# Denominators of a sketched attention from extra sketch columns instead of extra matmuls, and no early squares on GpSimd

## The chip, the cores and the metric

The kernel runs on one core of one Trainium2 chip. The metric is device time in microseconds (us) of one launch. Runs come with a state; a run more than 1.5% above the fastest of its kernel is called slow and is left out of comparisons.

## The reference, cut to what matters

Four batches of a polynomial-sketch attention (4 heads, 1088 positions, head size 32, r = 8) feed a feed-forward layer (FFN) with a squared ReLU.

```python
def phi(x):                         # q and k: 64 features per position
    a = np.einsum('rd,bhsd->bhsr', S1, x)
    b = np.einsum('rd,bhsd->bhsr', S2, x)
    return np.einsum('bhsi,bhsj->bhsij', a, b).reshape(*x.shape[:-1], r * r)
q_p, k_p = phi(q), phi(k)
kv = np.einsum('bhsf,bhsd->bhfd', k_p, v)
z = np.sum(k_p, axis=2)
num = np.einsum('bhsf,bhfd->bhsd', q_p, kv)
den = np.einsum('bhsf,bhf->bhs', q_p, z)[..., None] + 1e-06
x = num / den                       # 4352 tokens of 128
h = np.maximum(x @ w_in, 0.0)       # 2048 wide
out = h * h @ w_out
```

The identity behind the change: the denominator is the sum over i of a_i times the sum over j of z_ij b_j. The inner sum is linear in q, so it can be had from eight more columns of the q sketch, with weights z times S2.

## The kernel before

TensorE does a pair of matmuls per FFN block and token chunk: `pg` (x times w_in, one record in the trace) and `po` (times w_out, float32, two records); at 384 tokens they take 0.17 and 0.65 us of the chain. ScalarE does the ReLU (`gt`), and ScalarE, VectorE or, early on, GpSimd the square (`g`). Meanwhile each batch's attention is prepared. A small list scheduler in the kernel (`O`) fixes the order of instructions on each engine at build time from estimated durations. The path of a batch is: `kT`, `kc`, `fs`, `kp`, `ks` (k features) - `kvp` (kv and z) - `kvt`, copies `kv`, `z` on GpSimd; and `qT`, `qc` (q sketch) - `qb`, `qa` shuffles out of PSUM - `qp` products - `nd` (numerators and denominators) - `dT`, `dn`, `rd`, `bc` - `xT`.

```python
def a_kvr(b, h):                                   # GpSimd, per head
    ...
    for c in range(4):
        nc.gpsimd.tensor_copy(_ap(st[b, "kv"], 32 * c, 32, 64 * h, ...), _ap(st["kvt"], ...))
        nc.gpsimd.tensor_copy(_ap(zs[b % 2], 32 * c, 32, 64 * h + 8 * c, ...), _ap(st["kvt"], ...))

def a_qc(b, i0, nb):                               # q sketch, 16 small matmuls
    sketch(st[b, "qc", i0], qT, 32 * i0, 8 * nb, sf[:, 64:96])   # columns 16-31 of sf's part are zero

def a_nd(b, i0, nb, nd=None, col=0):
    ...                                            # numerators: 32 matmuls, kv x qp
    for o_, m0, w in dens(m):                      # denominators: z x qp
        for e in range(E):
            for h in range(H):
                nc.tensor.matmul(nd[32 * h : 32 * h + 32, col + o_ : col + o_ + w],
                                 z[:, o : o + 32], st[b, "qp", i0, e][:, ...], ...)

def a_dn(b, i0, nb):                               # VectorE: transpose, + eps, reciprocal
    ...

# squares: the first on VectorE, then ScalarE or VectorE, and GpSimd too for u < 9
{"DVE": dve(w)} if u < ND else {"ACT": 0.095 + w / 1200, "DVE": dve(w), **PS[u < NP]}

# bulk loads of batch b (k, v, q)
s0 = tu[first_unit[b - 1, 0]] - 8.0 if b > 1 else 0.0
```

A float32 matmul is two records in these traces, so the 16 calls of `sketch` show as `qc` x32.

Of the kernel before, what the change touches and what calls it, by code (L numbers as in the profile page):

```python
# [14 lines left out]
def _ap(t: bass.AP, p0: int, np_: int, off: int, free):  # L15
    p = list(t.ap)[0]
    return bass.AP(
        t.tensor, t.offset + p0 * p[0] + off, [[p[0], np_]] + [list(d) for d in free]
    )


class _Order:
# [30 lines left out]
    def run(self, hop=0.25):  # L53
        free = {}
        todo = list(self.ops)
        for op in todo:
            for e in op["engs"]:
                free.setdefault(e, 0.0)
        t = 0.0
        while todo:  # L60
            later, done = [], []
            for e in free:
                if free[e] > t:
                    later.append(free[e])
                    continue
                best = None
                for op in todo:
                    if e not in op["engs"] or op["start"] is not None:
                        continue
                    if any(d["end"] is None for d in op["deps"]):  # L70
                        continue
                    if any(d["start"] is None or d["start"] >= t for d in op["soft"]):
                        continue
                    r = op["at"]
                    for d in op["deps"]:
                        r = max(r, d["end"] + (0.0 if d["eng"] == e else hop + op["lag"]))
                    r += op["late"].get(e, 0.0)
                    if r > t:
                        later.append(r)
                    elif best is None or op["key"] < best["key"]:  # L80
                        best = op
                if best is not None:
                    best["start"], best["eng"] = t, e
                    best["end"] = free[e] = t + best["engs"][e]
                    done.append(best)
                    later.append(free[e])
            if done:
                todo = [op for op in todo if op["start"] is None]
            t = min((x for x in later if x > t), default=t + 0.01)
            assert t < 1000.0, [op["name"] for op in todo][:20]  # L90
        for op in sorted(self.ops, key=lambda op: (op["start"], op["n"])):
            op["emit"](op["eng"])
# [3 lines left out]
def kernel(  # L96
# [19 lines left out]
    GT, G2, LA = 4, 6, 3.5  # L116
    LU = 4
    W0, W3 = 10, 3
    ND, WI, KL = 1, (2.0, 4.0), (30.0, 8.0)



# [30 lines left out]
    kT, qT = sb("kT", SP), sb("qT", SP)  # L153
    w_in32, w_o, w_in = sb("w_in32", 2048), sb("w_o", 2048), sb("w_in", 2048, F32R)
    s_nat, s_T = sb("s_nat", 32, rows=32), sb("s_T", 32, rows=32)
    zs = [sb(f"z{i}", 64 * H) for i in range(2)]


    def load_k(eng, b, c0=0, c1=S):
# [256 lines left out]

    def a_rep_z(t_, col):
        nc.vector.tensor_tensor(
            out=_ap(zs[0], 0, 128, 0, [[32, 4], [128, 2], [1, 32]]),
            in0=_ap(t_, 0, 128, col + 32, [[512, 4], [64, 2], [1, 32]]),  # L420
            in1=_ap(own_c, 0, 128, 0, [[0, 4], [0, 2], [1, 32]]),
            op=mult,
        )


    def a_kvr(b, h):
        if h == 0:
            st[b, "kv"] = bpool.tile([128, 64 * H], F32, tag="kv", name="kv")
        for c in range(4):
            nc.gpsimd.tensor_copy(  # L430
                _ap(st[b, "kv"], 32 * c, 32, 64 * h, [[32, E], [1, 32]]),
                _ap(st["kvt"], 32 * h, 32, 0, [[64, E], [1, 32]]),
            )
            nc.gpsimd.tensor_copy(  # L434
                _ap(zs[b % 2], 32 * c, 32, 64 * h + 8 * c, [[32, E], [1, 8]]),
                _ap(st["kvt"], 32 * h, 32, 32, [[64, E], [1, 8]]),
            )

    def a_qc(b, i0, nb):
        st[b, "qc", i0] = att("qc")  # L440
        sketch(st[b, "qc", i0], qT, 32 * i0, 8 * nb, sf[:, 64:96])

    def a_qs(b, i0, nb, which, x):
        m = 8 * nb
# [24 lines left out]
    def a_nd(b, i0, nb, nd=None, col=0):  # L469
        m = 8 * nb  # L470
        nd = att("nd") if nd is None else nd
        st[b, "nd", i0] = nd, col
        kv, z = st[b, "kv"], zs[b % 2]
        for e in range(E):
            qp = st[b, "qp", i0, e]
            ch = [(c, h) for c in range(4) for h in range(H)]
            for c, h in ch:
                r, o = slice(32 * c, 32 * c + 32), 64 * h + 32 * e
                nc.tensor.matmul(  # L479
                    nd[32 * h : 32 * h + 32, 512 * c + col : 512 * c + col + m],  # L480
                    kv[r, o : o + 32], qp[r, m * h : m * h + m],
                    start=(e == 0), stop=(e == 1),
                )
        for o_, m0, w in dens(m):
            for e in range(E):
                for h in range(H):
                    o = 64 * h + 32 * e
                    nc.tensor.matmul(  # L488
                        nd[32 * h : 32 * h + 32, col + o_ : col + o_ + w],
                        z[:, o : o + 32], st[b, "qp", i0, e][:, m * h + m0 : m * h + m0 + w],  # L490
                        start=(e == 0), stop=(e == 1),
                    )

    def dens(m):
        if m < 256:
            return [(m, 0, m)]
        return [(m, 0, 160), (512 + m, 160, m - 160)]

    def a_dn(b, i0, nb):
        m = 8 * nb  # L500
# [69 lines left out]
    def square(u, eng):  # L570
        w = units[u][3] * units[u][5]
        g2 = fpool.tile([128, 512], F32, tag="g2", bufs=G2, name="g2")
        gt = st["gt", u]
        if eng == "ACT":
            nc.scalar.activation(g2[:, 0:w], gt[:, 0:w], Square)  # L575
        else:
            {"DVE": nc.vector, "POOL": nc.gpsimd}[eng].tensor_tensor(out=g2[:, 0:w], in0=gt[:, 0:w], in1=gt[:, 0:w], op=mult)  # L577
        g2s[u] = g2

    def ffn2(u, i, xs=None):  # L580
# [94 lines left out]
            _ap(iden, 32 * h, 32, 32 * h, [[0, 4], [1, 32]]),  # L675
        )
    nc.gpsimd.memset(_ap(vn[1], 96, 32, 32 * (NT - 2), [[32 * NT, H], [1, 64]]), 0.0)
    nc.gpsimd.memset(zs[1][:], 0.0)

    a_kT0(4, 3)  # L680
    a_kT0(7, 2)
# [99 lines left out]
    def q_tasks(b, i0, nb, key):  # L781
# [4 lines left out]
        if True:  # L786
            for x in range(2):
                i1, n1 = i0 + x * (nb // 2), nb // 2
                n1 = min(n1, G - i1)
                names.append(("qT", b, i1))  # L790
                O.add(
                    names[-1], {"DVE": dve(32 * n1)}, k0 - 1.5,
                    ([("qn", b)] if b else []) + prev["qTuse"], on(a_qT, b, i1, n1),
                )
        O.add(
            ("qc", b, i0), {"PE": 0.75}, k0 - 1.0, names, on(a_qc, b, i0, nb),
            rings=[("att", 1)], lag=PEL,
        )
        prev["qTuse"] = [("qc", b, i0)] if i0 + nb == 4 * NT else []
        for w_ in ("qb", "qa0", "qa1"):  # L800
            for x in range(2):
                O.add(
# [13 lines left out]
    def nd_tasks(b, i0, nb, key):  # L816
        m = 16 * nb
        qps = [("qp", b, i0, e, x) for e in range(E) for x in range(2)]
        O.add(
            ("nd", b, i0), {"PE": 0.7 + 2.5 * max(nb, 14) / 36}, key - 3.5 - 4 * dve(m), [("kvr", b, h) for h in range(H)], on(a_nd, b, i0, nb),  # L820
            uses=qps + [("qp", b, i0, 0, 0)], rings=[("att", 1)], lag=PEL,
        )
        O.add(
            ("dn", b, i0), {"DVE": 0.65 + m / 960 / 2 + 0.07 * len(dens(m // 2))}, key - 3.0 - 4 * dve(m), [], on(a_dn, b, i0, nb),
            uses=[("nd", b, i0)],
        )
        for x in range(2):
            O.add(
                ("bc", b, i0, x), {"DVE": dve(m)}, key - 2.5 - 4 * dve(m) + 0.1 * x, [], on(a_bc, b, i0, nb, x),
                uses=[("dn", b, i0)], rings=[("bc", 1)] if x == 0 else [],  # L830
            )
            O.add(
                ("x", b, i0, x), {"DVE": dve(m)}, key - 2.0 - 4 * dve(m) + 0.1 * x, [], on(a_x, b, i0, nb, x),
# [9 lines left out]

    prev["qTuse"] = []
    def k_tasks(b, k0, ks_lead):
        s0 = tu[first_unit[b - 1, 0]] - 8.0 if b > 1 else 0.0
        O.add(
            ("ld", b), {"SP": 1.0}, s0,
            [("qT", b - 2, 0), ("qT", b - 2, 18), ("kvs", b - 2), ("kT", b - 2, 18)]
            if b > 1 else [], on(loads, b), at=s0,  # L850
        )
        for x, y, t in (("ld", "kn", 6.0), ("kn", "vn", 3.0), ("vn", "qn", 3.0)):
            O.add((y, b), {"IO": t}, s0, [(x, b)], lambda eng: None)
# [26 lines left out]
    def kv_tasks(b, k0):  # L880
# [2 lines left out]
            uses=[("kp", b, h) for h in range(H)], rings=[("att", 1)], lag=PEL,  # L883
        )
        O.add(
            ("kvt", b), {"DVE": 0.2}, k0 + 1.0, [("kvr", b - 1, 3)], on(a_kvt, b),
            uses=[("kvs", b)],
        )
        w = [("nd", b - 2, i) for i, _ in AC[b - 2]] if b > 1 else []
        for h in range(H):  # L890
            O.add(
                ("kvr", b, h), {"POOL": 1.7}, k0 + 2.0 + 0.1 * h, w + [("kvt", b)],
                on(a_kvr, b, h),
            )

# [5 lines left out]
    chunk(q_tasks, 0, 1, 0.0)  # L901
    chunk(nd_tasks, 0, 1, 0.0)
    k_tasks(1, d1 - KL[0], KL[1])
    chunk(q_tasks, 0, 2, 2.0)
    chunk(nd_tasks, 0, 2, 2.0)
    for b in range(1, B):
        d = due(b, 0) - M
        if b > 1:
# [4 lines left out]

    pe1, pe2 = [], []
    ends = (NU - 2, NU - 1)
    PS, NP = ({}, {"POOL": 1.6}), 9
    for u in range(NU):
        b, ci, c0, n, d0, m = units[u]
        w = n * m
# [6 lines left out]
        for i in range(m):  # L926
# [8 lines left out]
        )  # L935
        O.add(
            ("sq", u),
            {"DVE": dve(w)} if u < ND else {"ACT": 0.095 + w / 1200, "DVE": dve(w), **PS[u < NP]},
            tu[u] - 0.6, [],
            lambda eng, u=u: square(u, eng), uses=[("relu", u)], rings=[("g2", G2)],  # L940
            late={"DVE": 0.0, "ACT": 0.2 if u > 1 else 0.0},
# [63 lines left out]
```

## Time and profile before

| | before |
|---|---|
| time, median of the three first runs | 194.36 us (193.66 to 196.87) |
| span of the profiled run | 192.5 us |
| busy share of TensorE / ScalarE / VectorE / GpSimd | 96% / 78% / 57% / 15% |
| TensorE in the chain that ended last | 91% of the span |

In the page, L and a number is a line of the kernel; `out<-in` names tiles. The busy spans of TensorE overlap (a `pg` of 384 tokens is shown for 0.63 us from 84.41 us on, and the next `po` starts at 84.88), so the pace of the `po` matmuls in the chain says more than the share: 0.17 + 0.65 = 0.82 us per pair at 384 tokens, and no wait of TensorE is listed after 46.66 us.

### The profile page before, as it was taken

The numbers are of one execution on the slowest core, as the hardware profiler recorded it, in microseconds if no ns is written. First come the engines' busy times: TensorE is split into PE (matmuls) and PEld (weight loads), VectorE is DVE, ScalarE is ACT, GpSimd is POOL, SyncE is SP. The second block draws the span as 40 slices with busy tenths as digits, with TensorE's granted clock in tenths as the row PEclk, the third lists the DMA queues.
The fourth block names the chain that finished last, engine by engine and source line by source line (L and its number), as shares of the span: only waits on it lengthen the run. The fifth ranks groups of instructions, "written<-read, shape, count | busy, mean of one in ns | idle before, by whom it ended". The sixth has DMA issues, their size and how long they took to land.

```text
span 192.5 us, 4309 instructions
## 1 busy us (share of the span) xinstructions
PE 185.5 (96%) x1682; PEld 124.2 (65%) x1683; DVE 109.6 (57%) x250; ACT 149.8 (78%) x329; POOL 28.3 (15%) x125
## 2 busy tenths in 40 slices
PE   8999999998999999999999999999999999999991
PEld 2756766663655656656677666656677755666891
DVE  4779879746949459359295892259293421222300
ACT  3418688875948889979589899879588988999970
POOL 2725000008700000083000000083000000000000
PEclk9999999999999999999999999999999999999999
DMA  5799500391020020167002020110003010030110
GB/s 178 186 348 294 135 3 2 45 293 45 0 44 0 12 36 0 24 160 209 3 2 46 0 34 0 25 19 0 3 0 46 15 19 2 0 48 0 25 20 27
DMA packets 24412, 11.29 MB, mean 59 GB/s; under 512 B 17864, under 2 KB 22728, under 8 KB 24392
## 3 DMA queue, kind: packets, MB, share of 16 engines
q1 hardware_dynamic: 23940, 10.82, 23.6%
q8 instruction: 13, 0.21, 0.4%
q10 hardware_dynamic: 452, 0.20, 0.4%
q14 instruction: 7, 0.06, 0.1%
HBM read 8.78 MB, written 2.23 MB: 57 GB/s over the span
## 4 chain that ended last, share of the span: by engine, by line
PE 91%; DVE 4%; DMA 1%; issue 1%; ACT 0%; POOL 0%; ACTq 0%; DVEq 0%
PE po L596 57%; PE pg L558 16%; PE nd L479 3%; PE nd L488 2%; PE kvp L381 2%; PE pol L591 2%; PE po L591 2%; DMA s_nat<-in_S_dram 1%; PE qc L283 1%; PE kvp L363 1%; PE kf L293 1%; PE kc L283 1%; DVE qp L462 1%; DVE qa L447 1%; DVE qT L276 1%
## 5 line engine op out<-in xcount | busy, mean ns | idle before, releaser
L596 PE MATMUL po<-g,w_o 128*128 128x384 f32 (+3 forms) x352 | 138.8, 479 | 1.4 <-issue 0.9
L558 PE MATMUL pg<-xT,w_in 128*128 128x384 f32 (+3 forms) x192 | 110.0, 582 | 0.3 <-DVE xT L751 0.3
L567 ACT ACTIVATE gt<-pg 128x384 f32<-128x384 f32 (+4 forms) x177 | 85.2, 490 | 24.6 <-PE pg L558 22.4
L596 PEld LDWEIGHTS po<-g,w_o 128*128 128x128 f32 x352 | 62.3, 189 | 24.1 <-issue 9.6
L575 ACT ACTIVATE g<-gt 128x384 f32<-128x384 f32 (+3 forms) x138 | 71.6, 532 | 3.2
L558 PEld LDWEIGHTS pg<-xT,w_in 128*128 128x128 f32 x192 | 36.0, 189 | 24.9 <-issue 6.1
L577 DVE TENSOR_TENSOR g<-gt 128x384 f32<-128x384 f32 (+4 forms) x37 | 20.9, 565 | 37.2 <-ACT gt L567 37.1
L430 POOL COPY kv<-kvt 32x64 f32<-32x64 f32 x48 | 11.5, 240 | 92.8 <-DVE kvt L399 91.0
L462 DVE TENSOR_TENSOR qp<-qa,qb 128x576 f32<-128x576 f32 (+2 forms) x20 | 12.1, 666 | 0.0
L447 DVE STREAM_SHUFFLE qa<-qc 128x576 f32<-128x576 f32 (+2 forms) x20 | 11.5, 650 | 0.0
L434 POOL COPY z<-kvt 32x16 f32<-32x16 f32 x48 | 10.3, 215 | 0.0
L600 DVE STREAM_TRANSPOSE oT<-po 128x384 f32<-128x384 f32 (+3 forms) x11 | 6.2, 564 | 5.4 <-PE po L596 5.3
L334 DVE TENSOR_TENSOR kp<-fs 128x576 f32<-128x576 f32 x12 | 8.2, 738 | 0.0
L479 PE MATMUL nd<-qp,kv 32*32 32x288 f32 (+2 forms) x320 | 7.0, 354 | 0.2 <-DVE qp L462 0.2
L325 DVE STREAM_TRANSPOSE fs<-kc 128x576 f32<-128x576 f32 x6 | 4.3, 761 | 4.5 <-PE kc L283 4.5
L504 DVE STREAM_TRANSPOSE dT<-nd 128x128 f32<-128x128 f32 (+2 forms) x8 | 2.2, 304 | 7.0 <-PE nd L488 7.0
L479 PEld LDWEIGHTS nd<-qp,kv 32*32 32x32 f32 x320 | 3.7, 103 | 3.5 <-issue 1.2
L447 DVE STREAM_SHUFFLE qb<-qc 128x576 f32<-128x576 f32 (+2 forms) x10 | 5.9, 642 | 0.0
L518 DVE STREAM_TRANSPOSE bc<-rd 128x576 f32<-128x576 f32 (+2 forms) x10 | 5.7, 610 | 0.2
L591 PE MATMUL pol<-w_o,g 128*128 128x128 f32 x32 | 5.7, 275 | 0.0
L276 DVE STREAM_TRANSPOSE qT<-qn 128x192 f32<-128x192 f32 (+3 forms) x11 | 5.7, 557 | 0.0
L639 PE MATMUL warm<-const-bfloat16-1.0 128*128 128x512 bf16 x12 | 4.9, 557 | 0.8 <-PEq L989 0.8
(90 smaller groups left out, 101.2 us busy)
## 6 DMA issues: line engine op xcount, KB each, us to landing
kn<-in_k_dram SPq DMA_DIRECT2D x3, 544.0 KB, 6.5
qn<-in_q_dram SPq DMA_DIRECT2D x3, 544.0 KB, 6.8
vn<-in_v_dram SPq DMA_DIRECT2D x9, 144.0 KB, 6.6
out_dram<-oT SPq DMA_DIRECT2D x24, 48.0 KB, 1.9
w_in<-in_moe_w_in_dram SPq DMA_DIRECT2D x4, 256.0 KB, 5.8
w_o<-in_moe_w_out_dram SPq DMA_DIRECT2D x4, 256.0 KB, 6.0
out_dram<-oT SPq DMA_DIRECT2D x8, 56.0 KB, 1.9
qn<-in_q_dram SPq DMA_DIRECT2D x1, 416.0 KB, 5.7
```

The lines of the kernel that those rows point to most:

```text
L334: nc.vector.tensor_tensor(out=_ap(st[b, "kp"], 0, 128, 2 * o, [[64, NT], [8, 8], [1, 8]]), in0=_ap(fs, 0, 128, o, [[32, NT], [1, 8], [0, 8]]),
L430: nc.gpsimd.tensor_copy(_ap(st[b, "kv"], 32 * c, 32, 64 * h, [[32, E], [1, 32]]), _ap(st["kvt"], 32 * h, 32, 0, [[64, E], [1, 32]]),)
L434: nc.gpsimd.tensor_copy(_ap(zs[b % 2], 32 * c, 32, 64 * h + 8 * c, [[32, E], [1, 8]]), _ap(st["kvt"], 32 * h, 32, 32, [[64, E], [1, 8]]),)
L447: nc.vector.stream_shuffle(in_=banks(st[b, "qc", i0], 2 * x, 0, m), out=_ap(st[b, which, i0], 0, 128, 2 * m * x, [[m, 2], [1, m]]), mask=m ...
L462: nc.vector.tensor_tensor(out=st[b, "qp", i0, e][:, r], in0=st[b, f"qa{e}", i0][:, r], in1=st[b, "qb", i0][:, r], op=mult,)
L479: nc.tensor.matmul(nd[32 * h : 32 * h + 32, 512 * c + col : 512 * c + col + m], kv[r, o : o + 32], qp[r, m * h : m * h + m], start=(e == 0 ...
L558: nc.tensor.matmul(st["pg", u][:, n * i : n * i + n], w_in[:, 128 * (d0 + i) : 128 * (d0 + i) + 128], st[b, "xT"][:, c0 : c0 + n],)
L567: nc.scalar.activation(gt[:, 0:w], st["pg", u][:, 0:w], Relu)
L575: nc.scalar.activation(g2[:, 0:w], gt[:, 0:w], Square)
L577: {"DVE": nc.vector, "POOL": nc.gpsimd}[eng].tensor_tensor(out=g2[:, 0:w], in0=gt[:, 0:w], in1=gt[:, 0:w], op=mult)
L591: nc.tensor.matmul(po[x // 128][:, 0:128], g[:, x : x + 128], w, start=(d == 0), stop=(d == NB - 1),)
L596: nc.tensor.matmul(po[0][:, 0:n], w, g, start=(d == 0), stop=(d == NB - 1))
```

## The change

The intent: take the denominator matmuls of batches 1 to 3 off TensorE, and take GpSimd's early squares away. VectorE makes the weights `sw` (z times S2, summed over j), `qc` yields a and the weighted sum in the same 32 columns, VectorE transposes them (`qt`), multiplies (`pd`), sums (`dn`) and inverts (`rc`), and GpSimd regroups the reciprocals to the partitions of their position blocks (`rd`). Batch 0 keeps its z matmuls.

```diff
-            nc.gpsimd.tensor_copy(_ap(zs[b % 2], ...), _ap(st["kvt"], ...))
-        sketch(st[b, "qc", i0], qT, 32 * i0, 8 * nb, sf[:, 64:96])
+        sketch(st[b, "qc", i0], qT, 32 * i0, 8 * nb, sw[b % 2] if b else sf[:, 64:96])
+    def a_w(b):      # pw = kvp(z columns) * S2; sw[:, 16:24] = reduce(pw)
+    def a_qt(b, x):  # qt = transposes of qc
+    def a_pd(b):     # pd = qt[0:8] * qt[16:24]   (a ninth column holds 1e-6)
+    def a_rc(b):     # dn = reduce(pd); rc = 1 / dn
+    def a_rl(b, c):
+        for h in range(H):
+            nc.gpsimd.tensor_copy(st[b, "rd", 0][32*h:32*h+32, NT*c:NT*c+NT],
+                                  st[b, "rc"][32*c:32*c+32, NT*h:NT*h+NT])
-        for o_, m0, w in dens(m):
+        for o_, m0, w in dens(m) if b == 0 else ():
-    ND, WI, KL = 1, (2.0, 4.0), (30.0, 8.0)
+    ND, QT, WI, KL, QL = 2, 3.0, (1.5, 3.0), (30.0, 12.0), 4.0
-            {"ACT": 0.095 + w / 1200, "DVE": dve(w), **PS[u < NP]},
+            {"ACT": 0.095 + w / 1200, "DVE": dve(w)},
-        s0 = tu[first_unit[b - 1, 0]] - 8.0 if b > 1 else 0.0
+        s0 = tu[first_unit[b - 1, 0]] - 4.0 if b > 1 else 0.0
-            [("qT", b - 2, 0), ("qT", b - 2, 18), ("kvs", b - 2), ("kT", b - 2, 18)]
+            [("nd", b - 1, 0)] if b > 1 else [], on(loads, b), at=s0,
...              (further: a look-ahead rule LOOK for VectorE, task entries and estimates for the scheduler)
```

So beside the new denominators the change retunes the order: squares off GpSimd, a second first square on VectorE, `qT` of the third chunk later, other leads, later bulk loads.

More of the change, by code (lines that the diff above doesn't have):

```diff
@@ L19, in _ap @@
     )
+LOOK = 0.5
 class _Order:
@@ L65, in run @@
                     continue
-                best = None
+                best, wait = None, []
                 for op in todo:
@@ L79, in run @@
                         later.append(r)
+                        wait.append((r, op["key"]))
                     elif best is None or op["key"] < best["key"]:
                         best = op
+                if best is not None and e == "DVE" and any(
+                    k < best["key"] and r < t + LOOK * best["engs"][e] for r, k in wait
+                ):
+                    continue
                 if best is not None:
@@ L155 @@
     s_nat, s_T = sb("s_nat", 32, rows=32), sb("s_T", 32, rows=32)
-    zs = [sb(f"z{i}", 64 * H) for i in range(2)]
+    z0 = sb("z0", 64 * H)
+    sw = [sb(f"sw{i}", 32) for i in range(2)]
+    pd = sb("pd", 9 * 4 * NT)
     def load_k(eng, b, c0=0, c1=S):
@@ L418, in a_rep_z @@
         nc.vector.tensor_tensor(
-            out=_ap(zs[0], 0, 128, 0, [[32, 4], [128, 2], [1, 32]]),
+            out=_ap(z0, 0, 128, 0, [[32, 4], [128, 2], [1, 32]]),
             in0=_ap(t_, 0, 128, col + 32, [[512, 4], [64, 2], [1, 32]]),
@@ L433, in a_kvr @@
             )
-            nc.gpsimd.tensor_copy(
-                _ap(zs[b % 2], 32 * c, 32, 64 * h + 8 * c, [[32, E], [1, 8]]),
-                _ap(st["kvt"], 32 * h, 32, 32, [[64, E], [1, 8]]),
-            )
     def a_qc(b, i0, nb):
         st[b, "qc", i0] = att("qc")
-        sketch(st[b, "qc", i0], qT, 32 * i0, 8 * nb, sf[:, 64:96])
+        sketch(st[b, "qc", i0], qT, 32 * i0, 8 * nb, sw[b % 2] if b else sf[:, 64:96])
+    def a_w(b):
+        pw = wpool.tile([128, 64], F32, tag="pw", bufs=1, name="pw")
+        nc.vector.tensor_tensor(
+            out=pw[:, :],
+            in0=_ap(st[b, "kvp"], 0, 128, 32, [[64, E], [8, 4], [1, 8]]),
+            in1=_ap(sf, 0, 128, 72, [[0, E], [0, 4], [1, 8]]),
+            op=mult,
+        )
+        nc.vector.tensor_reduce(
+            out=sw[b % 2][:, 16:24], in_=_ap(pw, 0, 128, 0, [[8, 8], [1, 8]]), op=add, axis=AX
+        )
+    def a_qt(b, x):
+        if x == 0:
+            st[b, "qt"] = wpool.tile([128, 32 * NT * H], F32, tag="qt", bufs=1, name="qt")
+        m = 32 * NT
+        nc.vector.transpose(
+            _ap(st[b, "qt"], 0, 128, 2 * m * x, [[m, 2], [1, m]]),
+            banks(st[b, "qc", 0], 2 * x, 0, m),
+        )
+    def a_pd(b):
+        qt = st[b, "qt"]
+        nc.vector.tensor_tensor(
+            out=_ap(pd, 0, 128, 0, [[9, 4 * NT], [1, 8]]),
+            in0=_ap(qt, 0, 128, 0, [[32, 4 * NT], [1, 8]]),
+            in1=_ap(qt, 0, 128, 16, [[32, 4 * NT], [1, 8]]),
+            op=mult,
+        )
+    def a_rc(b):
+        dn = wpool.tile([128, 4 * NT], F32, tag="dn", name="dn")
+        nc.vector.tensor_reduce(
+            out=dn[:, :], in_=_ap(pd, 0, 128, 0, [[9, 4 * NT], [1, 9]]), op=add, axis=AX
+        )
+        st[b, "rc"] = wpool.tile([128, 4 * NT], F32, tag="rc", bufs=1, name="rc")
+        nc.vector.reciprocal(st[b, "rc"][:, :], dn[:, :])
+    def a_rl(b, c):
+        if c == 0:
+            st[b, "rd", 0] = wpool.tile([128, 4 * NT], F32, tag="rd", name="rd")
+        for h in range(H):
+            nc.gpsimd.tensor_copy(
+                st[b, "rd", 0][32 * h : 32 * h + 32, NT * c : NT * c + NT],
+                st[b, "rc"][32 * c : 32 * c + 32, NT * h : NT * h + NT],
+            )
     def a_qs(b, i0, nb, which, x):
@@ L472, in a_nd @@
         st[b, "nd", i0] = nd, col
-        kv, z = st[b, "kv"], zs[b % 2]
+        kv, z = st[b, "kv"], z0
         for e in range(E):
@@ L494, in dens @@
     def dens(m):
-        if m < 256:
-            return [(m, 0, m)]
-        return [(m, 0, 160), (512 + m, 160, m - 160)]
+        return [(m, 0, m)]
     def a_dn(b, i0, nb):
@@ L576, in square @@
         else:
-            {"DVE": nc.vector, "POOL": nc.gpsimd}[eng].tensor_tensor(out=g2[:, 0:w], in0=gt[:, 0:w], in1=gt[:, 0:w], op=mult)
+            nc.vector.tensor_tensor(out=g2[:, 0:w], in0=gt[:, 0:w], in1=gt[:, 0:w], op=mult)
         g2s[u] = g2
@@ L677 @@
     nc.gpsimd.memset(_ap(vn[1], 96, 32, 32 * (NT - 2), [[32 * NT, H], [1, 64]]), 0.0)
-    nc.gpsimd.memset(zs[1][:], 0.0)
+    for w in sw:
+        nc.gpsimd.tensor_copy(w[:, :], sf[:, 64:96])
+    nc.gpsimd.memset(_ap(pd, 0, 128, 8, [[9, 4 * NT], [1, 1]]), 1e-6)
     a_kT0(4, 3)
@@ L793, in q_tasks @@
                     ([("qn", b)] if b else []) + prev["qTuse"], on(a_qT, b, i1, n1),
+                    at=QT if i0 == 20 else 0.0,
                 )
         O.add(
-            ("qc", b, i0), {"PE": 0.75}, k0 - 1.0, names, on(a_qc, b, i0, nb),
+            ("qc", b, i0), {"PE": 0.75}, k0 - 1.0, names + [("w", b)], on(a_qc, b, i0, nb),
             rings=[("att", 1)], lag=PEL,
@@ L799, in q_tasks @@
         prev["qTuse"] = [("qc", b, i0)] if i0 + nb == 4 * NT else []
+        if b:
+            for x in range(2):
+                O.add(
+                    ("qt", b, x), {"DVE": dve(m)}, k0 - 0.3 + 0.1 * x, [], on(a_qt, b, x),
+                    uses=[("qc", b, i0)], rings=[("qt", 1)] if x == 0 else [],
+                )
+            O.add(
+                ("pd", b), {"DVE": dve(m // 2)}, k0 - 0.1, [("rc", b - 1)], on(a_pd, b),
+                uses=[("qt", b, 0), ("qt", b, 1)],
+            )
+            O.add(
+                ("rc", b), {"DVE": 0.8}, k0 - 0.1, [], on(a_rc, b), uses=[("pd", b)],
+                rings=[("rc", 1)],
+            )
+            for c in range(4):
+                O.add(
+                    ("rl", b, c), {"POOL": 0.8}, k0 + 0.1 * c, [], on(a_rl, b, c),
+                    uses=[("rc", b)], rings=[("rd", 2)] if c == 0 else [],
+                )
         for w_ in ("qb", "qa0", "qa1"):
@@ L819, in nd_tasks @@
         O.add(
-            ("nd", b, i0), {"PE": 0.7 + 2.5 * max(nb, 14) / 36}, key - 3.5 - 4 * dve(m), [("kvr", b, h) for h in range(H)], on(a_nd, b, i0, nb),
+            ("nd", b, i0), {"PE": 1.65 if b else 0.7 + 2.5 * max(nb, 14) / 36}, key - 3.5 - 4 * dve(m), [("kvr", b, h) for h in range(H)], on(a_nd, b, i0, nb),
             uses=qps + [("qp", b, i0, 0, 0)], rings=[("att", 1)], lag=PEL,
         )
-        O.add(
-            ("dn", b, i0), {"DVE": 0.65 + m / 960 / 2 + 0.07 * len(dens(m // 2))}, key - 3.0 - 4 * dve(m), [], on(a_dn, b, i0, nb),
-            uses=[("nd", b, i0)],
-        )
+        if b == 0:
+            O.add(
+                ("dn", b, i0), {"DVE": 0.72 + m / 960 / 2}, key - 3.0 - 4 * dve(m), [],
+                on(a_dn, b, i0, nb), uses=[("nd", b, i0)],
+            )
         for x in range(2):
@@ L829, in nd_tasks @@
                 ("bc", b, i0, x), {"DVE": dve(m)}, key - 2.5 - 4 * dve(m) + 0.1 * x, [], on(a_bc, b, i0, nb, x),
-                uses=[("dn", b, i0)], rings=[("bc", 1)] if x == 0 else [],
+                uses=[("dn", b, i0)] if b == 0 else [("rl", b, 2 * x), ("rl", b, 2 * x + 1)],
+                rings=[("bc", 1)] if x == 0 else [],
             )
@@ L845, in k_tasks @@
     def k_tasks(b, k0, ks_lead):
-        s0 = tu[first_unit[b - 1, 0]] - 8.0 if b > 1 else 0.0
+        s0 = tu[first_unit[b - 1, 0]] - 4.0 if b > 1 else 0.0
         O.add(
             ("ld", b), {"SP": 1.0}, s0,
-            [("qT", b - 2, 0), ("qT", b - 2, 18), ("kvs", b - 2), ("kT", b - 2, 18)]
-            if b > 1 else [], on(loads, b), at=s0,
+            [("nd", b - 1, 0)] if b > 1 else [], on(loads, b), at=s0,
         )
@@ L885, in kv_tasks @@
         O.add(
+            ("w", b), {"DVE": 0.3}, k0 + 0.9, [], on(a_w, b), uses=[("kvs", b)],
+        )
+        O.add(
             ("kvt", b), {"DVE": 0.2}, k0 + 1.0, [("kvr", b - 1, 3)], on(a_kvt, b),
@@ L891, in kv_tasks @@
             O.add(
-                ("kvr", b, h), {"POOL": 1.7}, k0 + 2.0 + 0.1 * h, w + [("kvt", b)],
+                ("kvr", b, h), {"POOL": 0.95}, k0 + 2.0 + 0.1 * h, w + [("kvt", b)],
                 on(a_kvr, b, h),
@@ L903 @@
     k_tasks(1, d1 - KL[0], KL[1])
-    chunk(q_tasks, 0, 2, 2.0)
-    chunk(nd_tasks, 0, 2, 2.0)
+    chunk(q_tasks, 0, 2, QL)
+    chunk(nd_tasks, 0, 2, QL)
     for b in range(1, B):
@@ L915 @@
     ends = (NU - 2, NU - 1)
-    PS, NP = ({}, {"POOL": 1.6}), 9
     for u in range(NU):
@@ L937 @@
             ("sq", u),
-            {"DVE": dve(w)} if u < ND else {"ACT": 0.095 + w / 1200, "DVE": dve(w), **PS[u < NP]},
+            {"DVE": dve(w)} if u < ND else
+            {"ACT": 0.095 + w / 1200, "DVE": dve(w)},
             tu[u] - 0.6, [],
```

## The prediction

> **What bounds the kernel now.** I read the page from the top: busy shares, slices, then the chain that ended last.
>
> ```profile
> PE 185.5 (96%) x1682; PEld 124.2 (65%) x1683; DVE 109.6 (57%) x250; ACT 149.8 (78%) x329; POOL 28.3 (15%) x125
> ...
> PE   8999999998999999999999999999999999999991
> ...
> PE 91%; DVE 4%; DMA 1%; issue 1%; ACT 0%; POOL 0%; ACTq 0%; DVEq 0%
> PE po L596 57%; PE pg L558 16%; PE nd L479 3%; PE nd L488 2%; PE kvp L381 2%; PE pol L591 2%; PE po L591 2%; DMA s_nat<-in_S_dram 1%; PE qc L283 1%; PE kvp L363 1%; PE kf L293 1%; PE kc L283 1%; DVE qp L462 1%; DVE qa L447 1%; DVE qT L276 1%
> ```
>
> TensorE is busy in every slice and carries 91% of the chain. Busy alone would not prove it, since matmuls overlap, so I checked the pace. [...] in the chain, `po` recurs every 0.82 us from 84 to 92 us. From about 57 us on TensorE therefore runs at its own pace, and only work taken off it shortens the end. What lies between FFN pairs shows in the chain in order of time:
>
> ```profile
> 92.40 0.65 PE po L596 x2
> 93.19 1.53 PE nd L479 x63
> 94.72 1.12 PE nd L488 x32
> 95.84 0.84 PE po L596 x2
> ```
>
> Batch 2 pays 1.53 us for the numerators (L479), then 1.12 us for the denominators (L488). Batches 1 and 3 show the same 1.12.
>
> Earlier the picture differs. From 14 to 24 us the chain leaves TensorE for VectorE (`qT`, `g`, `qb`, `qa`, `qp`), and the timeline shows why that stretch is slow (start, length, engine line op, operands, count):
>
> ```profile
> 15.22 0.61 POOL L577 TENSOR_TENSOR g<-gt 128x256 f32<-128x256 f32 x1 [3.64 <-ACT gt L567]
> 15.32 0.79 DVE L577 TENSOR_TENSOR g<-gt 128x256 f32<-128x256 f32 x1
> ...
> 17.70 2.41 DVE L462 TENSOR_TENSOR qp<-qa,qb 128x192 f32<-128x192 f32 x4
> 17.89 1.05 POOL L577 TENSOR_TENSOR g<-gt 128x512 f32<-128x512 f32 x1 [1.31 <-ACT gt L567]
> 18.89 0.74 POOL L632 CAST w_in<-w_in 128x512 fp32r<-128x512 f32 x1
> 19.89 0.71 PE L479 MATMUL nd<-qp,kv 32*32 32x96 f32 x32 [0.20 <-DVE qp L462]
> ```
>
> and the groups with shapes kept apart (busy us, then mean ns):
>
> ```profile
> L462 DVE TENSOR_TENSOR qp<-qa,qb 128x192 f32<-128x192 f32 x4 | 2.4, 660 | 0.0
> L462 DVE TENSOR_TENSOR qp<-qa,qb 128x256 f32<-128x256 f32 x4 | 1.4, 409 | 0.0
> ```
>
> Four products of 192 columns took 2.41 us, longer than four of 256 columns (1.4) with GpSimd idle. Each slow VectorE product lies beside a GpSimd square or cast.
>
> [...] 660 ns against 409 above, while the shuffles out of PSUM at 15.8-16.6 us, beside a cast, keep their 368 ns. [...] The trace has 13 packets of 16 KB on an instruction queue, and one wait of TensorE for nothing else, inside one matmul right after the kvp and qc bursts:
>
> ```profile
> 46.66 0.59 PE L596 MATMUL po<-g,w_o 128*128 128x384 f32 x1 [0.93 <-issue]
> ```
>
> **The change, part by part.**
>
> 1. *Removed from TensorE:* the z matmuls of batches 1 to 3 (192 - 96 = 96 of 128 go; the two chunks of batch 0 keep 32 in all). In the chain each batch loses 1.12 us: 3 x 1.12 = 3.36 us, all on the path. The denominator columns ride in columns 16-23 of the sketch weights, zero before, so the 32 `qc` matmul records per batch stay the same size: +0.
>
> 2. *Added to VectorE per batch:* two `qt` transposes of 1152 columns, like `fs`, 1.45 us for the pair; the product `pd` over 288 columns, about 0.37 (qp: 409 ns at 256, starts closer than that); a reduction over 324, about 0.4 (estimate from the same slope); a reciprocal over 36, 0.38; product and reduction for `sw` over 64 columns, about 0.2 each (small operations take 0.17-0.24). Sum 3.0. Removed: `dT` 0.55, `dn` 0.19, reciprocal 0.38: 1.1. Net about +1.9 us x 3. VectorE is at 57%, so the total is no issue; the place is. From `qc` to `nd` it now needs 1.45 + 0.37 + 0.4 + 0.35 + 6 shuffles at 0.70 (start to start) + 4 products at 0.69 = 9.5, with hand-overs about 10.0 us. The instruction order of the changed kernel puts between `qc` and `nd` 8 pairs of 448 and 3 of 384 in batch 1, about 8 x 0.95 + 3 x 0.82 = 10.1 us; about 10.4 us in batches 2 and 3. It just fits; and `nd` begins with the first two products only, 0.7 us of further slack. I count 0 to 0.2 us lost per batch.
>
> 3. *`qc` now waits for `sw`, hence for kvp.* The order leaves two `po` and one or two `pg` between: 1.45 to 1.6 us. Before, `kvt` started 0.14 us after kvp; with 0.2 + 0.2 + 0.32 for `sw` and `kvt`, `qc` could go after about 1.0 us. Fits; 0 to 0.1 per batch.
>
> 4. *GpSimd:* 16 z copies per batch (215 ns) go, 16 of 32x9 come, about 0.2 each = 3.2 us. They follow `rc`, and `bc` wants them only after shuffles and products (7 us later): hidden, as only PSUM shuffles run beside them.
>
> 5. *No squares on GpSimd; two early squares on VectorE; the second half of `qT` after `qp`.* The products lose their contention: 4 x (0.60 - 0.30) = 1.2 us, and the first square 0.4. Following the order: first `po` at about 15.75 instead of 16.21; `nd` at about 18.6 instead of 19.24 and without its wait inside; the first 384-token `pg` at about 22.1 instead of 23.3. I book 1.1 us.
>
> 6. *ScalarE* takes more squares while VectorE is full. ReLU and square of a 384-unit take 0.93 us from start to start against 0.82 on TensorE. Over 10 us of FFN it falls behind by 10 x 0.13 = 1.3 us; the lead of four units is 3.3 us, less 1.3 for one unit's own latency: 2.0. It holds, and `nd` (1.53) lets it catch up.
>
> 7. *The instruction wait of 0.93 us* lies behind a burst that stays. I count half: 0.3 gained.
>
> Sum: 3.36 + 1.1 + 0.3 - 0.5 (parts 2, 3) = 4.3 us; 194.3 - 4.3 = 190.0.
>
> **The rivals.** (a) *VectorE becomes the bound between `qc` and `nd`.* For: the slack of batch 1 is nothing on paper. Against: `nd` starts on half its input. If the new operations take 1 us more than estimated, three stalls of about 0.7 give back 2 us: 192. (b) *ScalarE becomes the bound* as VectorE takes no square for 13 us per batch. For: 0.93 against 0.82, and 78% busy. Against: `nd`, `qc` and kvp give it 3.5 us of rest per batch. If so, back 1 to 2 us: 191.5. (c) *The early stage gains nothing* because ScalarE, now without GpSimd's help, sets the pace there: then 191.1. (d) *Better:* the instruction wait vanishes and nothing stalls: 188.7.
>
> **Range and chances.** The 3.36 us is nearly certain as work, the 1.1 us likely; new waits can only take away. I put 190.0, and 188.6 to 191.9 eight times in ten. Two per cent of 194.3 is 3.9 us, close to my 4.3: faster by over 2% 0.56, within 2% 0.42, slower 0.02.
>
> **What would show it.** Right: in the chain, `nd` of batches 1 to 3 takes 1.5 us and is followed at once by `po`; the four 192-column `qp` mean about 0.35 us; the first 384-token `pg` starts near 22 us. Step 2 is wrong if TensorE shows a wait for `qp` at `nd`; step 3 if it waits for `sw` at `qc`; step 6 if `po` waits for ScalarE's `g` and the `po` cadence after `qc` exceeds 0.82 us; step 5 if that early `pg` stays near 23 us. The prediction as a whole fails if such waits add to over 2 us, or if TensorE's small-matmul bursts meet more instruction waits than before.

## The result, and the profile after

The changed kernel took 189.24 us in the median (189.21 to 189.63, four fast runs); before took 195.0 (193.66 to 196.87, four runs, one of them slow). A ratio is computed as the mean time of one kernel's fast runs over the mean of the other's in the same rounds, so it is not quite the ratio of the medians: here 0.9731, interval 0.9667 to 0.9796, which is faster. The output is correct.

The page after, busy shares and chain:

```profile
PE 182.0 (97%) x1586; PEld 121.8 (65%) x1587; DVE 115.0 (61%) x261; ACT 149.4 (80%) x329; POOL 28.0 (15%) x125
...
PE 94%; DMA 2%; DVE 1%; issue 0%; ACT 0%; POOL 0%; ACTq 0%; DVEq 0%
```

TensorE lost 96 matmul records and is still nearly the whole chain, now 94%; VectorE's share in the chain fell from 4% to 1%, although its busy time rose by 5.4 us. The same stretch as in the prediction, chain in order of time (start, length, what):

```profile
90.82 0.65 PE po L653 x2
91.46 1.53 PE nd L538 x63
93.00 0.34 PE pg L615
```

The numerators take their 1.53 us, and the FFN follows at once. The early stretch in the chain, first before, then after:

```profile
14.26 1.13 DVE qT L276 x4
15.39 0.66 DVE g L577
...
17.80 2.05 DVE qp L462 x3
...
19.89 0.71 PE nd L479 x30
```

```profile
15.40 0.44 PE pg L615 x2
15.84 0.43 PE po L653 x2
...
19.01 0.89 PE nd L538 x52
19.90 0.47 PE nd L547 x16
20.37 0.32 PE pg L615
```

The chain no longer leaves TensorE after 14 us, and the first 384-token `pg` comes in the timeline at 22.52 us instead of 23.30.

The instructions, one by one, show where this early gain arises. (1) The first `po` starts 0.53 us earlier, at 15.68 instead of 16.21 us. In before, its square `g` on VectorE stood behind four `qT` transposes and took 792 ns beside a square on GpSimd (15.22 to 15.83 us); after, it stands behind two of them and takes 426 ns. By the difference of the two durations, 0.37 of the 0.53 us come from the square on GpSimd (an estimate). (2) 0.23 us are lost again at a `pg` that follows a ReLU. (3) At `nd`, 0.41 us are gained: its matmuls with `kv` lasted 1.37 us in before, with a wait of 0.20 us for `qp` inside, and last 0.96 us now. In sum 0.71 us at the next `po`.

To see where the time went, I compared the start of the same `po` matmul in two traces. Both kernels run all 416 `po` and `pol` records in the same order, so the difference at a given one is what has been gained up to there, if both have done the same attention work by then; the rows are such places (between them the `kc`, `kvp` and `qc` of the two orders stand at different units, and the difference swings by up to 2.2 us). The second trace of before is the first experiment below.

| at this po | before minus after, us | second trace of before minus after, us |
|---|---|---|
| the first | 0.53 | 0.51 |
| second of 384 tokens (28.7 us after) | 0.77 | 0.68 |
| the last of the first 384-token chunk, after qc of batch 1 (44.4 us) | 0.78 | 0.69 |
| the one after it (45.2 us) | 2.08 | 0.80 |
| after nd of batch 1 (54.6 us) | 3.20 | 1.92 |
| after nd of batch 2 (93.2 us) | 4.28 | 3.00 |
| after nd of batch 3 (135.4 us) | 5.31 | 4.02 |
| the last | 5.21 | 3.93 |

There are three steps: about 0.7 us by the end of the early stage, a jump of 1.3 us at one matmul (in the first trace of before only), and 1.12, 1.08 and 1.03 us at the three `nd`. From row to row nothing is given back before the end (0.1 us).

### The profile page after: what moved, and what is told of

Same layout as the page of the kernel before. It is cut to its first block, busy times and chain, and to the rows that moved or that the text cites. A ratio compares the mean times of both kernels' runs of the same rounds, so it can differ in the third digit from the quotient of the medians.

```text
span 187.4 us, 4142 instructions
## 1 busy us (share of the span) xinstructions
PE 182.0 (97%) x1586; PEld 121.8 (65%) x1587; DVE 115.0 (61%) x261; ACT 149.4 (80%) x329; POOL 28.0 (15%) x125
## 4 chain that ended last, share of the span: by engine, by line
PE 94%; DMA 2%; DVE 1%; issue 0%; ACT 0%; POOL 0%; ACTq 0%; DVEq 0%
PE po L653 60%; PE pg L615 18%; PE nd L538 3%; PE kvp L394 2%; PE pol L648 2%; PE po L648 2%; PE qc L296 2%; DMA s_nat<-in_S_dram 2%; PE kvp L376 1%; PE kf L306 1%; PE kc L296 1%; PE x L749 1%; PE nd L547 1%; PE den L795 0%; PE den L773 0%
## 5 line engine op out<-in xcount | busy, mean ns | idle before, releaser
L634 DVE TENSOR_TENSOR g<-gt 128x384 f32<-128x384 f32 (+4 forms) x39 | 21.4, 550 | 39.5 <-ACT gt L624 39.4
L521 DVE TENSOR_TENSOR qp<-qa,qb 128x576 f32<-128x576 f32 (+2 forms) x20 | 10.8, 601 | 0.0
L497 POOL COPY rd<-rc 32x9 f32<-32x9 f32 x48 | 8.9, 185 | 2.2
L469 DVE STREAM_TRANSPOSE qt<-qc 128x576 f32<-128x576 f32 x6 | 4.3, 762 | 5.5 <-PE qc L296 5.5
L584 DVE TENSOR_TENSOR xT<-nd,bc 128x576 fp32r<-128x576 f32 (+2 forms) x10 | 5.6, 596 | 0.8 <-PE nd L538 0.7
```

Of the source, the lines that this page charges most:

```text
L497: nc.gpsimd.tensor_copy(st[b, "rd", 0][32 * h : 32 * h + 32, NT * c : NT * c + NT], st[b, "rc"][32 * c : 32 * c + 32, NT * h : NT * h + NT],)
L521: nc.vector.tensor_tensor(out=st[b, "qp", i0, e][:, r], in0=st[b, f"qa{e}", i0][:, r], in1=st[b, "qb", i0][:, r], op=mult,)
L634: nc.vector.tensor_tensor(out=g2[:, 0:w], in0=gt[:, 0:w], in1=gt[:, 0:w], op=mult)
```

## The experiments

Twelve kernels ran, on two chips. The changed kernel itself took 188.93 to 189.54 us again in its fast runs on the first of these chips (mean 189.18). On the second it did not run itself; its trace and 189.2 us serve as the reference there.

### Is the 1.3 us jump a property of the kernel?

The kernel before, unchanged, one look.

> The kernel before, unchanged, for a second trace. Question: is the wait of TensorE inside one po matmul right after the kvp and qc bursts of batch 1 (about 1.3 us more than the other pairs there, and 0.93 us idle) a property of the kernel or an accident of one run? Theory L ([...] the bulk loads of batch 2 run at 37 to 43 us): it is there again, between 0.6 and 1.6 us. If accident: it is gone or at another place. The four 192-column qp products again average about 0.66 us.

192.98 us, correct; as a single run its state is unknown, but no other run of before was as fast. The wait is gone. The chain of the first trace of before, then that of the second:

```profile
45.21 0.52 PE po L596
45.73 0.93 issue
46.66 0.59 PE po L596
```

```profile
44.42 0.70 PE qc L283 x32
45.12 0.84 PE po L596 x2
```

In the first, TensorE stands still for 0.93 us between the two records of one matmul and waits for nothing that the profile shows. In the second the same matmul runs through (and the four 192-column `qp` again average 659 ns). So the wait belongs to an execution, not to the kernel. Six fast runs of before spread from 193.04 to 195.16 us, mean 194.10, which is 1.1 us above this run; waits of this kind would fit, but only this one was traced.

### Do the bulk loads cause that wait?

Before, with one part of the change: loads issued later.

```diff
-        s0 = tu[first_unit[b - 1, 0]] - 8.0 if b > 1 else 0.0
-            [("qT", b - 2, 0), ...] if b > 1 else [], on(loads, b), at=s0,
+        s0 = tu[first_unit[b - 1, 0]] - 4.0 if b > 1 else 0.0
+            [("nd", b - 1, 0)] if b > 1 else [], on(loads, b), at=s0,
```

> The kernel before with one part of the change: the k, v and q loads of batches 2 and 3 are issued later (after nd of the batch before). Theory L: no bulk load is running when TensorE enters the kvp and qc bursts of batch 1, [...] the wait is gone, and the time falls by about 1.2 us (0.6%). Rival B [...]: the wait stays at the same place and the time does not change (within 0.3 us).

Fast runs 193.0, 193.53, 193.98 (one slow, 198.86); ratio 0.9975, interval 0.9888 to 1.0062. The traced run has no wait, but neither has the second trace of before, and the two end within 0.06 us of each other at the last `po`. Inconclusive.

The changed kernel with the same lines the other way round, loads early:

> The changed kernel with the loads issued early again, as before; TensorE's order stays the same. Theory L: the wait returns near the kvp and qc bursts of batch 1 and the time rises by 0.6 to 1.5 us, to about 190.3. Rival B: no wait, 189.2 as for the changed kernel, since something else in its order spreads the bursts.

189.53 us in the median (189.1 to 189.9), mean 189.52 against 189.18 of the changed kernel. Its trace has a smaller wait near the same place:

```profile
44.35 0.20 PE pg L615
44.56 0.41 issue
44.97 0.91 PE po L653 x2
```

That spoke for the loads, though weakly: the mean rose by 0.34 us, where 0.6 to 1.5 was expected, and the fast runs of the two kernels overlap. So I put the cause in on purpose: the changed kernel with 3 MB of dummy loads right after the first output.

```diff
+        if (b, c0) == (0, 0):
+            for _ in range(3):
+                for c in range(4):
+                    load_wi(nc.sync, c)
```

> The changed kernel with 3 MB of dummy loads (the w_in weights into a buffer that nothing reads any more) issued right after the first output, so that bulk loads run from about 36 to 46 us, over the kvp and qc bursts of batch 1, on the same queue as the real loads. Theory L [...]: a wait of 0.3 to 2 us that follows no engine appears in TensorE between 38 and 47 us, [...] and the time and its spread rise (mean 189.5 to 191). Rival (the wait of before had another cause): no wait there, 189.2 as the changed kernel.

189.35 us (189.02 to 189.58, five fast runs, mean 189.31). The loads ran where they should, and TensorE did not stop. Stretches of the trace, with busy us of each engine, granted clock, share of the DMA engines and GB/s, then the chain:

```profile
37.00:40.00 3.00, 3.00 (x88) 2.21 (x86) 2.36 (x6) 2.84 (x8) 0.00 (x0) 1.00 0.84 281
40.00:43.00 3.00, 3.00 (x53) 1.59 (x43) 0.94 (x4) 1.42 (x4) 1.56 (x7) 1.00 0.88 263
```

```profile
38.93 1.25 PE kvp L394 x80
40.18 0.84 PE po L653 x2
...
41.84 0.70 PE qc L296 x32
```

With the DMA engines 84 to 88% busy over both bursts there is no wait. Theory L, that bulk loads alone cause it, falls in this form. The dummy loads are not the same as the real ones (packets of 2048 bytes, the real ones of 896 to 4352), but the second trace of before ran the real ones over the same stretch, up to 45 us, without a wait; and in the two executions with the wait the loads had ended over 1 us before TensorE stopped (at 44.5 and 42.8 us).

What else the traces show: in the two executions with the wait, a 16 KB packet on the instruction queue started after kvp, at 44.08 us in before (kvp ends at 43.26, qc starts at 44.44) and at 42.56 us in the early-loads kernel (qc ends at 42.46). In the second trace of before it started at 41.43 us, ahead of kvp, and in the run with dummy loads at 40.02, before kvp ended; neither waited. That these packets have to do with the wait is not shown: the two that came after kvp took 1.06 us and so had ended 0.6 and 0.9 us before TensorE stopped (at 45.73 and 44.56). That TensorE waited for instructions there, as "instruction wait" in the prediction has it, was the guess. The cause of the wait stays open.

### What do the z matmuls cost?

The changed kernel with the z matmuls of batches 1 to 3 back as dead work.

```diff
-        for o_, m0, w in dens(m) if b == 0 else ():
+        for o_, m0, w in dens(m):        # and dens() split as before
```

> The changed kernel, with the 96 z matmuls of batches 1 to 3 put back as dead work in the same PSUM columns as before (their result is not read; the output stays right). TensorE's order is otherwise the same. Theory (the removed matmuls are on the path at their full time): slower by 3 x 1.08 = 3.2 us, to about 192.4. Rival (part of them was hidden beside other waits): less than 2 us.

192.38 us (192.33 to 192.64), mean 192.43: 3.2 us more than the changed kernel. The same `po` shows +0.97 after nd of batch 1, then 2.09 and 3.19 (this run had started 0.16 us earlier), +3.18 at the end. The chain:

```profile
52.64 1.53 PE nd L538 x63
54.17 1.12 PE nd L547 x32
55.29 0.40 PE pg L617
```

The 1.12 us is back and counts in full. The rival, that part of it had been hidden, is out.

### Do the new denominators gain this without the retuning?

The new denominators with every setting of before: squares on GpSimd, early loads, LOOK = 0, old leads.

```diff
-LOOK = 0.5
+LOOK = 0.0
-    ND, QT, WI, KL, QL = 2, 3.0, (1.5, 3.0), (30.0, 12.0), 4.0
+    ND, QT, WI, KL, QL = 1, 0.0, (2.0, 4.0), (30.0, 8.0), 2.0
+    (loads and the GpSimd choice for u < 9 as in the kernel before)
```

> The new denominators alone, with all other settings of the kernel before (squares on GpSimd, early loads, no look-ahead rule, old leads). Theory (the parts add): 3.2 us faster than before, so about 191 us against 194.3, ratio about 0.983; the wait after the bursts of batch 1 stays, about 1.2 us. Rival (the new VectorE work needs the retuned order): TensorE waits at nd or qc and less than 2 us is gained.

190.18 us (189.89 to 190.44), ratio 0.9811 (0.9784 to 0.9839, by the 2% line unclear): the means of fast runs are 193.73 and 190.17 on this chip, 3.6 us. By the same `po`, its trace gains 3.1 us on the second trace of before from the first `po` to the last. So the denominators bring what the z matmuls cost, with the old settings, and TensorE waits for no product at `nd` in the later batches. The 1.3 us wait that I expected to stay was not in its trace, in line with its belonging to single executions. The retuning is worth about another 1.0 us, going by 189.2 us of the changed kernel from another chip.

### What did the squares do to the early stage?

The changed kernel with the early squares allowed on GpSimd again.

```diff
-    ND, ... = 2, ...
+    ND, ... = 1, ...
-            {"ACT": 0.095 + w / 1200, "DVE": dve(w)},
+            {"ACT": 0.095 + w / 1200, "DVE": dve(w), **({"POOL": 1.6} if u < 9 else {})},
```

> The changed kernel with the early squares allowed on GpSimd again and one instead of two first squares on VectorE. Theory (the early gain came from VectorE products no longer shut out by GpSimd): the 192-column qp products beside a GpSimd square slow from 0.35 to 0.5 to 0.7 us each, the first 384-token pg starts 0.4 to 0.9 us later, and the time rises by that, to about 189.9. Rival (the early gain comes from the later qT transposes and the order): no change, within 0.2 us.

190.17 us (190.14 to 190.56), mean 190.26: 1.0 us slower than the changed kernel. The `qp` of 192 columns and the waits in the chain:

```profile
L521 DVE TENSOR_TENSOR qp<-qa,qb 128x192 f32<-128x192 f32 x4 | 2.0, 562 | 0.0
```

```profile
16.77 0.58 ACT gt L624
17.35 0.14 issue
17.49 0.48 PE pg L615 x2
```

The products slow to 562 ns beside GpSimd's square, as expected, and the first 384-token `pg` comes 1.03 us later (23.55). But the loss is not the early gain undone. The first `po` comes at 15.71 us, 0.04 later than in the changed kernel, since here no GpSimd square stands beside the first square; and `nd` does not wait for `qp` (0.96 us, as in the changed kernel). The chain runs through ScalarE instead: who takes which square also decides when ScalarE comes to the next ReLU, and TensorE waits twice for one, 0.30 us each. So that the time rose is no proof of the theory: as far as the chain shows, GpSimd squares (and one first square fewer on VectorE, changed with them) cost 1.0 us in the new order by way of ScalarE, and not by the slow products.

So I made the contention alone: three GpSimd copies that nothing needs, after the last cast, and as a control three memsets.

```diff
+        if c == 3:
+            for _ in range(3):
+                nc.gpsimd.tensor_copy(scratch[:, :], w_in32[:, 0:512])    # control: nc.gpsimd.memset(scratch, 0.0)
```

> The changed kernel with three dummy GpSimd copies of 128x512 between buffers that nothing uses, right after the last cast, so that they run at about 17.4 to 19.2 us beside the four 192-column qp products (two SBUF inputs each). Nothing waits for them. Theory [...]: qp mean rises from 346 ns to 550 to 700, nd of the second chunk waits, the time rises by 0.2 to 0.7 us. Rival (the slow qp of before came from elsewhere): qp stay at 350 ns, no change.

189.04 us (188.87 to 189.11). The timeline and the group:

```profile
16.32 1.98 POOL L695 COPY scratch<-w_in 128x512 f32<-128x512 f32 x3
17.20 1.85 DVE L522 TENSOR_TENSOR qp<-qa,qb 128x192 f32<-128x192 f32 x4
```

```profile
L522 DVE TENSOR_TENSOR qp<-qa,qb 128x192 f32<-128x192 f32 x4 | 1.8, 520 | 0.0
```

The products slow from 346 to 520 ns in the mean, and there is nothing else on GpSimd there: the slowdown comes from the copies, which read SBUF and also write it. One by one, the first two products take 628 and 760 ns and end 0.21 us after the copy that they met (17.83 after 17.62, 18.51 after 18.30 us), and the other two take 346 and 344 ns. In before it was the same: two products of four took 1190 and 759 ns and ended 0.22 and 0.21 us after the square and the cast. But the time does not move. The four products now end at 19.05 us, and `nd` still starts in its place, since in the changed order they had room: they end at 18.47 us in the changed kernel, `nd` starts at 18.94 and wants the last of them in its second half. My expectation of 0.2 to 0.7 us was wrong. The same slowdown was on the path in before: there `nd` started at 19.24 us, `qp` ended at 20.11, and `nd` took 0.41 us longer.

> The same with three GpSimd memsets of 128x512, which write SBUF and read nothing. Theory [...]: qp stay near 350 ns and the time is that of the changed kernel. Rival (any GpSimd work slows VectorE): qp slow as with the copies.

Fast runs 189.05, 189.1, 189.33 us. The profile fell on a slow run (195.4 us), in which the memsets were over 5 us before `qp` came; its 352 ns say nothing. The control is inconclusive: whether writes alone slow such products is not shown.

### How much room has VectorE between qc and nd?

The changed kernel with `pd` made three times, then six times, per later batch (the same values).

```diff
+        for _ in range(2):        # or 5
+            nc.vector.tensor_tensor(out=..pd.., in0=..qt.., in1=..qt.., op=mult)
```

> The changed kernel with the pd product of each later batch made three times instead of once (the same values; about 0.9 us more on VectorE between qc and nd). From the trace of the changed kernel qp ends 0.2 us before nd starts in batch 1 and 0.5 us in batches 2 and 3, and the last qp is wanted only in the second half of nd, 0.7 us later. Theory (VectorE has slack of about 1 us there): under 0.4 us slower in all. Rival (VectorE is already the bound there): 0.6 to 0.9 us slower per batch, 2 to 2.7 in all.

189.1 us (189.06 to 189.13): no change. 0.95 us more on VectorE in each of three batches is free, although the last `qp` now ends 0.78 us after `nd` starts in batch 1 (53.42 and 52.64 us).

> The changed kernel with pd made six times per later batch, 5 x 0.475 = 2.4 us more on VectorE between qc and nd. Two more products cost nothing. From the trace of the changed kernel the last qp ends at 52.5 us in batch 1 and at 90.9 in batch 2, and is wanted in the second half of nd, at about 53.5 and 92.1. Theory (slack of 1.0 to 1.2 us per batch, then VectorE's time counts in full): the waits are 2.4 - 1.0 = 1.4 us in batch 1 and 1.2 in batches 2 and 3, so 3.8 us slower in all, to about 193, with the wait at nd for qp. Rival (TensorE is still covered by the scheduler's margin): under 1 us.

192.91 us in the median (one of four runs slow, 199.14); fast runs 192.73 to 193.0, mean 192.85, that is 3.7 us more (3.8 expected). By the same `po`: 1.5, 1.15 and 1.14 us at the three `nd`. The timeline of batch 1 shows the wait:

```profile
52.12 2.74 DVE L527 TENSOR_TENSOR qp<-qa,qb 128x576 f32<-128x576 f32 x4
53.00 2.68 PE L544 MATMUL nd<-qp,kv 32*32 32x288 f32 x64 [0.35 <-DVE qp L527]
```

`nd` follows the products step by step, and takes 2.68 us instead of 1.60 in this view. So VectorE's slack in the changed kernel lies between 0.95 and 2.4 us per batch; 2.4 us less what was lost gives about 0.9 in batch 1, where the 0.95 us thus just fitted, and 1.2 in batches 2 and 3.

### The changed kernel again

> The changed kernel, unchanged, on this chip, for comparison: 189.2, ratio to before about 0.973.

Fast runs 188.93, 189.06, 189.54; ratio 0.9739, as expected (interval 0.9673 to 0.9805, by the 2% line unclear, since the runs of before spread). One run, the profiled one, was slow (194.4 us). Compared by the same `po`, that trace is late by 5.16 us at the first `po` and by 5.16 us at the last: everything was lost before. The chain of its start, then that of the fast trace:

```profile
5.35 3.22 PE kf L306 x14
...
12.68 3.19 PE kvp L376 x56
```

```profile
5.32 1.75 PE kf L306 x14
...
9.34 1.78 PE kvp L376 x56
```

TensorE ran at about half pace from 5 to 16 us (`kf` 3.22 us against 1.75, `kvp` 3.19 against 1.78). The trace's own clock records agree with that: in the twelve other traces they begin, at full clock, between 3.9 and 5.9 us, in this one at 16.7 us, and in the slow trace of the memset kernel, which starts in the same way (`kf` 3.13 us), at 20.4 us. (The page shows a granted clock of 1.00 from the start, because it takes the time before the first record for full clock.) So in the two slow executions that were traced TensorE got its full clock 11 to 16 us late; why, no run shows. The slow runs of the other kernels, before included (198.84 and 199.88 us), lie 4.7 to 6.3 us above the means of their fast ones, but were not traced; the 196.87 us of the first rounds lies 2.3 us above and may be something else. Slow runs occur with both kernels, so they are not put down to the change.

None of the experiments gave a version that beats the changed kernel beyond noise.

## Why the prediction was right

The time, 189.24 us, lies in the stated range, and faster was the likelier outcome. The main term held; that the total came so near is partly luck, since step 5 was booked 0.3 to 0.4 us too high and steps 2 and 3 lost none of the 0.5 us booked for them. By its own steps:

1. *The z matmuls, 3.36 us on the path.* Right: 1.12 + 1.08 + 1.03 = 3.23 us in the traces, 3.2 us when put back.
2. *VectorE just fits between qc and nd, 0 to 0.2 us lost per batch.* Right, and the loss was 0. The sum was a little low in its new terms: `pd` took 474 ns (0.37 estimated), the reduction 491 (0.4). From the start of `qt` to the end of `qp`, batch 1 took 9.92 us (42.60 to 52.52). TensorE's work from the end of `qc` to `nd` took 10.3 us (10.1 predicted), so `qp` was done 0.2 us before `nd` began. The further slack, that `nd` begins with half its input, was not needed here; the threefold `pd` used it.
3. *`qc` waits for `sw`.* Right, no wait: `pw` 225 ns, `sw` 221, `kvt` 0.31 us, done at 40.97 us; `qc` starts at 41.65.
4. *GpSimd hidden.* Right: the 16 copies end at 49.2 us, `bc` starts at 52.94.
5. *Early stage, 1.1 us.* The direction was right, the size too large: 0.7 to 0.8 us. The predicted slow products are real (660 to 346 ns), and the first `po` came at 15.68 us (15.75 predicted), `nd` at 18.94 (18.6 predicted), the first 384-token `pg` at 22.52 (22.1 predicted). The first square lost its 0.4 us as predicted (792 to 426 ns). The step counted VectorE's 1.2 us as if `nd` followed it; but `nd` lost only 0.41 us to the slow products in before, and after, `qp` is done at 18.48 us while TensorE, with a wait for ReLU and its own FFN, comes to `nd` at 18.94.
6. *ScalarE holds.* Right in the later batches: the `po` cadence after `qc` stays at 0.82 us for 384 tokens, and its idle time before ReLU went from 24.6 to 20.0 us in all.
7. *The wait of 0.93 us, half of it, 0.3 us.* This term was mis-sized. It costs 1.3 us of pace in the trace of before, 0 in another execution of the same kernel; a mean share of about 1.1 us would fit the spread of before, but is not shown. The prediction took one execution's wait for a property of the kernel, and took the idle time of 0.93 us for its cost; and half of that is 0.47, not 0.3.

Three smaller slips change nothing: the records taken off are 128 - 32 = 96, not "192 - 96"; the chain is back on TensorE at 19.89 us, not at 24; and the terms of (d) give 188.9 (190.0, less 0.6 for the rest of the wait and 0.5), not 188.7.

The sum was 4.3 us. Measured were 5.2 us at the last `po` of the first two traces (5.1 in the spans): 3.2 + 0.8 + 1.3, less 0.1 at the end. Against the execution of before without the wait it is 3.9 (3.8 in the spans): 3.2 + 0.8, less 0.1. Rival (a) did not come, and the six-fold run shows how near it is; (b) and (c) did not come either, though the run with squares on GpSimd shows that ScalarE can set the pace there; (d), 188.7, named the right direction.

## What to carry to other kernels

Where one engine runs at its own pace, price a change by what it takes off that engine's stream, then check each queue that feeds it against the room that the order leaves: here 1.1 us of matmuls per batch were bought with some 2 us more of VectorE time, and VectorE kept about 1 us of room. A slow instruction seen in a trace costs only what the next wait shows: the same slowdown of `qp` by GpSimd cost 0.41 us at `nd` in the old order and nothing in the new. Before explaining a wait that follows no engine, look whether it is there in a second execution.
